# Fourteen output stores move from the sync queue to the GpSimd queue in a fused attention and maxout kernel

## The chip, the cores and the metric

The kernel runs on one core of one Trainium2 chip. The metric is the device time of one execution in microseconds; the time before is the median of three runs. The engines are named as in the profile: PE is TensorE, PEld its weight load, DVE VectorE, ACT ScalarE, POOL GpSimd, and SP the sync engine, which computes nothing and issues DMAs.

## The reference

Two layers are computed, one after the other. The first is attention for 8 batches, 8 heads, 576 tokens and a head size of 64, in which only scores near the row's maximum count:

```python
scores = scale * np.matmul(q, k.transpose(0, 1, 3, 2))
thresh = np.max(scores, axis=-1, keepdims=True) - tau      # tau = 0.02
scores = np.where(scores >= thresh, scores, -1000000000.0)
attn = np.exp(scores - np.max(scores, axis=-1, keepdims=True))
attn = attn / (np.sum(attn, axis=-1, keepdims=True) + 1e-09)
x = np.matmul(attn, v)            # then heads side by side: 4608 tokens x 512
```

The second works on the 4608 tokens with three weight matrices of 512 x 768 and one of 768 x 512:

```python
h = np.maximum(np.maximum(x @ w1, x @ w2), x @ w3)
out = h @ w_out                   # 4608 x 512, float32
```

## The kernel before

The work is cut into 16 "quads" (one batch, four heads). Each quad goes through nine chunks, and each chunk is two halves of 128 rows by 576 columns. PE makes the scores of a half in PSUM (`sc`, float32 operands `kt` and `qt` or `qs`). DVE takes a maximum or minimum of it and in the same instruction copies it into a buffer `z` in SBUF (`maximum`). ACT turns `z` into exponentials, and either ACT or DVE keeps those over the threshold and sums them (`exponents`, `numerators`). DVE inverts the two sums (`rs`). POOL multiplies each half of `z` by its `rs` into a bfloat16 tile `P` (`normalized`), which gives the `z` buffer back. When both halves of `P` are there, SP issues a DMA that transposes it into `ptq` (`turned`). When all nine chunks of a quad are turned, PE multiplies them with the values `vb` and `vrb` into `o` (`product`), and DVE or ACT copies that to `xt`.

The second layer follows one batch behind. PE makes the pieces `ph` (6 blocks of the hidden size by three matrices), ACT and DVE take their maximum (`hm`, `hT`), and PE multiplies by `w_out` into `po` (`outp`). A piece of `outp` makes two row blocks of 128 tokens; ACT copies each into one half of a tile `ob` of 128 x 2 x 512 (`done(a)`, a = 0 and 1). There are two `ob` buffers, so ACT fills one only after the store of the piece two before has landed. For whole batches one DMA then stores both halves; it writes rows of 4 KB and 512 KB in all. The function `done` does not issue it but puts it on the list `stores`. Seven of the eight batches are whole, with two pieces each, so there are 14 joined stores. The last batch is split and stores each half by itself.

Besides P, POOL casts the weights and the values (`w`, `wo`, `vb`, `vr`) and copies swapped halves of `qt` to `qs`, which PE needs for scores. SP issues nearly all DMAs: the loads of q, k and v, the weights, the 144 transposes and the stores. In the program each DMA of SP waits until the one eight before it has landed, since they share eight semaphores in turn.

The order of everything is written out by hand in the string `ORDER`, one letter per step. `S`, `T`, `O`, `F`, `N` start PE's pieces, `m`, `s`, `e`, `n`, `k`, `r` are the steps of the softmax, `p` one half of `P`, `t` its transpose, `u` the copy into `ob`, and `o` takes the next entry of the list `stores` and issues it. Each engine gets its instructions in the order of the letters (line 93 is the helper that records them, so nearly all rows of the profile have line 93) and waits only by semaphores. An instruction that waits holds up those behind it on its engine, DMA issues included. Nine buffers of `z` exist, and later two more are taken in turn from the weights' staging tiles; `P` has six.

Of the kernel before, what the change touches and what calls it, by code (L numbers as in the profile page):

```python
# [104 lines left out]
def kernel(  # L105
# [23 lines left out]
    tensor, scalar, vector, pool, sync = (  # L129
        _Ordered(tc, e) for e in (nc.tensor, nc.scalar, nc.vector, nc.gpsimd, nc.sync))  # L130
# [51 lines left out]
    def bank(name, where):  # L182
        return ps_s.tile([128, 1024], F32, name=name, tag=f"s{where}")
# [273 lines left out]
    def halves(banks):  # L457


        mine = []  # L460

        def issue(swap):
            if swap:

                gate = tensor.nop()
                tc.add_manual_dep(gate.ins, mine[0], mybir.DependencyInfo(mybir.DependencyClass.Sync, mybir.DependencyReason.DATA), reason="swap")
            for ms in zip(*banks):
                for h in (1, 0):
                    x = (1 - h) ^ swap
                    o, w, m = ms[x]  # L470
                    rows = slice(64 * h, 64 * h + 64)
                    last = tensor.matmul(o, w(rows), m(rows), start=(not swap and ms[x] is banks[x][0]),
                                         stop=(swap == 1 and ms[x] is banks[x][-1]))
            if not swap:
                mine.append(last.ins.name)

        return (lambda: issue(0)), (lambda: issue(1))

    def ffn(b, part):
# [46 lines left out]
        def outp(cs):  # L526

            my = {}
            c = cs[0]
            last = b == B - 1 and cs[-1] == 3  # L530

            def first(where):
                ps = bank("po", where)
                my["ps"] = two = [ps[:, 0:512], bank("po", (where + 2) % 4)[:, 512:1024] if last else ps[:, 512:1024]]
                if len(cs) == 1:
                    for f in range(NF):
                        tensor.matmul(ps[:, 0:512], h_of(b)[:, f, chunk_of(b, c)], wo[:, f, :],
                                      start=(f == 0), stop=(f == NF - 1))
                    return
                my["h"] = halves([[(two[a],  # L540
                                    lambda rows, a=a, f=f: h_of(b)[rows, f, chunk_of(b, c + gap * a)],
                                    lambda rows, f=f: wo[rows, f, :]) for f in range(NF)] for a in range(2)])
                my["h"][0]()

            def done(a):
                if a == 0:
                    my["ob"] = hp_.tile([128, 2, DM], F32, name="ob")
                both = my["ob"]
                ob = both[:, a]
                src = my["ps"][a]  # L550
                if last and a == 1:
                    vector.tensor_copy(out=ob, in_=src)
                    ends.append(lambda: scalar.dma_start(out=rows_out[:, (0, 2, 1, 3)[c + a]:8:4], in_=ob))
                    return
                scalar.activation(out=ob, in_=src, func=AF.Copy)
                if part is not None:
                    stores.append(lambda: sync.dma_start(out=rows_out[:, (0, 2, 1, 3)[c + a]:8:4], in_=ob))
                elif a == 1:
                    stores.append(lambda: sync.dma_start(
                        out=rows_out[:, 0:8].rearrange("p (x s a) m -> p x s (a m)", x=2, a=2)[:, :, c],  # L560
                        in_=both.rearrange("p a m -> p (a m)")))
            p = _Piece((b, "out", c), first, (lambda: my["h"][1]()) if len(cs) == 2 else None,
                       [lambda a=a: done(a) for a in range(len(cs))])
            p.kind = "uf" if last else "u"
            return p
# [76 lines left out]
    Ls, xts, stores, stores9, ends, ninths = {}, {}, [], [], [], []  # L642
# [10 lines left out]
    def h_of(b):  # L653

        return hT

    def chunk_of(b, c):
        o = S * (b % 2) + (64 if ninth_first(b) else 0) + 128 * c
        return slice(o, o + 128)
# [166 lines left out]
```

## Time and profile before

| | |
|---|---|
| time before, median of 3 runs | 447.56 us (447.33 to 448.41) |
| profiled execution, its time | 448.08 us |
| profiled execution, its span | 446.3 us |
| mean granted clock of TensorE | 0.991 |
| joined stores, issued by SP | 14, 512 KB each, 4.0 us median from issue to landing |
| transposes, issued by SP | 144, 4.2 us median to landing |
| share of DMA time on the queue of SP | 94.9% of 16 engines |

The span is the time between the first and the last instruction of the profiled execution; its time has 1.8 us more around it. Busy times are sums by engine. A row of a group gives the engine, the operation, the tile written and the tiles read, the shapes, the count, and then the busy time, the mean duration and the idle time of the engine just before. A row of the timeline gives the start, the duration, the instruction, how many of its kind follow one another, and in brackets the idle time before it with what ended it. The time in which an engine issues a DMA is not counted as busy.

### The profile page before, as it was taken

What the parts mean: (1) busy time and instruction counts of PE and PEld (TensorE: products, weight loads), DVE (VectorE), ACT (ScalarE), POOL (GpSimd) and SP (SyncE); (2) the same over time, 40 slices, a digit from 0 to 9 for tenths busy, and PEclk for the clock granted to TensorE, in tenths of its full rate; (3) what the DMA queues carried; (4) which work ended last, traced back from release to release, by engine and by line L of the source; (5) the groups of instructions that cost most, each with busy time, mean ns of one, the idle gap of its engine ahead of it and who ended that gap; (6) DMA issues with size and microseconds to landing.
All of it is one profiled execution on the core that took longest, in us unless ns stands there. A gap on an engine that the chain in (4) does not pass through costs nothing.

```text
span 446.3 us, 14304 instructions
## 1 busy us (share of the span) xinstructions
PE 421.6 (94%) x5214; PEld 319.6 (72%) x5214; DVE 393.8 (88%) x1228; ACT 403.3 (90%) x836; POOL 312.8 (70%) x420
## 2 busy tenths in 40 slices
PE   6866779999999999999999999999999999999995
PEld 5544347787788767787687777788688786787972
DVE  4788999989999999999999999998999998899541
ACT  4999999999999999999999999899999999987532
POOL 2799889979878687686785877676677676457300
PEclk9899999999999999999999999999999999999999
DMA  7999999999999999699899999989999976487723
GB/s 196 270 290 195 288 186 252 227 219 250 205 231 207 213 239 284 120 245 170 143 236 184 228 209 206 206 166 222 196 201 201 235 147 113 75 175 134 176 85 108
DMA packets 213959, 88.50 MB, mean 198 GB/s; under 512 B 189184, under 2 KB 202240, under 8 KB 213888
## 3 DMA queue, kind: packets, MB, share of 16 engines
q1 hardware_dynamic: 213360, 86.96, 94.9%
q8 instruction: 41, 0.67, 0.6%
q10 hardware_dynamic: 528, 0.62, 0.5%
q14 instruction: 30, 0.25, 0.2%
HBM read 35.65 MB, written 9.44 MB: 101 GB/s over the span
## 4 chain that ended last, share of the span: by engine, by line
PE 77%; DVE 7%; ACT 5%; DMA 4%; issue 3%; POOL 3%; SPq 0%; POOLq 0%; DVEq 0%; ACTq 0%
PE ph L93 29%; PE sc L93 26%; PE po L93 10%; PE o L93 8%; DVE z L93 5%; ACT z L93 4%; PE tp L93 3%; POOL P L93 1%; DMA vr<-in_v_dram 1%; DMA stage<-in_moe_w_dram 1%; DMA k<-in_k_dram 1%; POOL qs L93 1%; SPq L93 0%; DVE xt L93 0%; DVE hm L93 0%
## 5 line engine op out<-in xcount | busy, mean ns | idle before, releaser
L93 POOL TENSOR_SCALAR P<-z,rs 128x576 bf16<-128x576 f32 x250 | 201.0, 815 | 63.9 <-DVE rs L93 27.2
L93 DVE TENSOR_SCALAR_CACHE_REDUCE z<-sc 128x576 f32<-128x576 f32 x250 | 183.7, 750 | 14.8 <-PE sc L93 8.7
L93 PE MATMUL sc<-kt,qs 64*128 64x256 f32 (+2 forms) x640 | 180.9, 418 | 7.7 <-DVE z L93 2.4
L93 PE MATMUL sc<-kt,qt 64*128 64x320 f32 (+2 forms) x640 | 181.0, 428 | 4.8 <-ACT z L93 2.9
L93 PE MATMUL ph<-xt,w 64*128 64x288 bf16 (+2 forms) x2160 | 170.8, 283 | 0.1
L93 PEld LDWEIGHTS <-w 64*128 64x128 bf16 (+1 forms) x2160 | 129.8, 94 | 29.1 <-issue 4.7
L93 ACT ACTIVATE z<-z 128x576 f32<-128x576 f32 x174 | 117.7, 679 | 0.1
L93 PEld LDWEIGHTS sc<-kt,qs 64*128 64x128 f32 (+1 forms) x640 | 91.7, 178 | 27.2 <-DVE z L93 5.5
L93 ACT ACTIVATE z<-z,th 128x576 f32<-128x576 f32 x143 | 106.1, 768 | 5.2 <-DVE th L93 4.8
L93 PEld LDWEIGHTS sc<-kt,qt 64*128 64x128 f32 (+1 forms) x640 | 91.2, 178 | 19.2 <-ACT z L93 6.1
L93 DVE SCALAR_TENSOR_TENSOR z<-z 128x576 f32<-128x576 f32 x76 | 63.0, 840 | 0.2
L93 PE MATMUL po<-wo,hT 64*128 64x512 bf16 (+2 forms) x480 | 53.8, 355 | 0.3
L93 POOL COPY qs<-qt 64x640 f32<-64x640 f32 (+3 forms) x66 | 43.5, 660 | 10.8 <-ACT qt L93 7.2
L93 ACT ACTIVATE z<-z,nm 128x576 f32<-128x576 f32 x68 | 50.6, 767 | 0.0
L93 DVE TENSOR_TENSOR hm<-ph,hm 128x576 bf16<-128x576 f32 (+2 forms) x54 | 37.0, 686 | 9.3 <-PE ph L93 8.9
L93 ACT ACTIVATE hm<-ph 128x576 bf16<-128x576 f32 (+2 forms) x54 | 31.7, 588 | 13.5 <-PE ph L93 13.0
L93 POOL TENSOR_SCALAR P<-stage,rs 128x576 bf16<-128x576 f32 x38 | 30.3, 802 | 19.1 <-ACT z L93 5.4
L93 PEld LDWEIGHTS <-hT 64*128 64x128 bf16 (+1 forms) x480 | 29.8, 95 | 17.0 <-issue 2.5
L93 DVE TENSOR_TENSOR hT<-ph,hm 128x576 bf16<-128x576 f32 (+2 forms) x54 | 37.0, 686 | 4.0 <-PE ph L93 2.3
L93 PE MATMUL o<-ptq,vb 128*64 128x64 bf16 (+2 forms) x544 | 39.0, 281 | 0.1
L93 ACT ACTIVATION_READ_ACCUMULATOR z<-z 128x1 f32 x174 | 34.3, 197 | 0.0
L93 PEld LDWEIGHTS <-vb 128*64 128x64 bf16 x544 | 23.4, 111 | 12.9 <-issue 5.1
(45 smaller groups left out, 433.1 us busy)
## 6 DMA issues: line engine op xcount, KB each, us to landing
vm<-in_v_dram SPq DMA_DIRECT2D x32, 256.0 KB, 4.5
qm<-in_q_dram SPq DMA_DIRECT2D x15, 512.0 KB, 5.2
km<-in_k_dram SPq DMA_DIRECT2D x15, 512.0 KB, 5.2
out_dram<-ob SPq DMA_DIRECT2D x14, 512.0 KB, 4.0
stage<-in_moe_w_dram SPq DMA_DIRECT2D x9, 512.0 KB, 4.8
ptq<-P SPq DMA_TRANSPOSE x144, 4.2
vr<-in_v_dram SPq DMA_DIRECT2D x16, 128.0 KB, 3.8
stage<-in_moe_w_out_dram SPq DMA_DIRECT2D x3, 512.0 KB, 5.2
```

The source lines that it names most:

```text
L93: ins = fn(*a, **kw)
```

## The change

The joined stores are issued by POOL's queue in place of SP's. The letters of `ORDER` stay as they are, so a store now stands among POOL's instructions, where the letter `o` falls between the letters `p`, `q`, `y` and `z` of POOL, and no longer among SP's loads and transposes. The stores of the split last batch and of the ninth blocks (`ob9`) stay where they were.

```diff
                 if part is not None:
                     stores.append(lambda: sync.dma_start(out=rows_out[:, (0, 2, 1, 3)[c + a]:8:4], in_=ob))
                 elif a == 1:
-                    stores.append(lambda: sync.dma_start(
+                    stores.append(lambda: pool.dma_start(
                         out=rows_out[:, 0:8].rearrange("p (x s a) m -> p x s (a m)", x=2, a=2)[:, :, c],
                         in_=both.rearrange("p a m -> p (a m)")))
```

In the program's order POOL has 14 DMAs more and SP 14 fewer; PE, DVE and ACT keep their instructions and their order. The first store on POOL stands between the two halves of one `P`. The wait of ACT for a free `ob` buffer is now for a DMA of POOL's queue.

## The prediction

> **What bounds the kernel now.** I read the page's busy table first, then the busy time by stretch, the rows of the moved DMA, and the timelines of POOL and DVE around each place where a moved store will stand.
>
> ```profile
> PE 421.6 (94%) x5214; PEld 319.6 (72%) x5214; DVE 393.8 (88%) x1228; ACT 403.3 (90%) x836; POOL 312.8 (70%) x420
> ```
>
> ```profile
> 0.00:118.00 118.00, 99.47 (x1082) 69.16 (x1084) 102.58 (x316) 108.72 (x230) 98.22 (x132) 0.97 1.10 235
> 118.00:428.00 310.00, 308.78 (x4026) 242.45 (x4023) 284.76 (x901) 290.38 (x599) 214.56 (x289) 1.00 0.95 190
> ```
>
> The columns of the second fence are the stretch, its length, busy PE, PEld, DVE, ACT and POOL, then the PE clock, the DMA share and GB/s. All fourteen moved stores lie in the second stretch, between 120.23 and 426.64 us on SP. There PE is idle for 1.2 us of 310, so whatever delays a score or a hidden piece there pushes the end; POOL is idle for 95 us, in gaps. A store on POOL is therefore free where a gap follows it before anyone needs POOL's next output, and is paid where none does.
>
> ```profile
> L93 SPq DMA_TRANSPOSE ptq<-P x144: 1241/1426/4436, 16.8 to 419.4; - x144
> L93 SPq DMA_DIRECT2D out_dram<-ob x26: 538/602/767, 120.2 to 442.1; - x26
> L93 POOL CAST vb<-vm 128x1024 bf16<-128x1024 f32 x16 | 17.4, 1090 | 3.8 <-DMA vm<-in_v_dram 2.6 <-PE ph L93 1.1
> ```
>
> The first two rows are issues on SP's queue (min/median/max ns), the third POOL's cast of a tile of the stored tile's shape (busy us, mean ns).
>
> **What is removed.** SP loses 14 issues of 0.60 us, 8.4 us. The waits of SP's queue are 136.6 us for POOL's P (93 times), so SP mostly stands waiting for POOL, and what it gains at a store it spends at its next transpose. After 118 us PE's list of waits has none for a DMA of over 0.3 us. I cost the relief at nothing; the cover is that wait for P. What it could bring at most is POOL's waits on DMAs after 118 us, 0.6 us for `vb` and 0.6 us for a P.
>
> **What is added: one issue on POOL, 14 times.** No row of this trace shows a DMA issued by POOL. The bounds are 0.60 us (the same DMA on SP) and 1.86 us (POOL's longest P row). The nearest row of POOL's own for a full 128-partition tile is the cast, 1.03 us undisturbed (at 225.43) and 1.09 on the mean; with the 0.06 to 0.10 us that POOL leaves between two instructions of different kinds I take 1.2 us.
>
> The Trainium skill (DMA: Bandwidth & Descriptors, Specifications) gives a first byte after about 1 us on the GpSimd path and about 0.6 us on the sync and scalar path. The second figure agrees with the 0.60 us row here; the first is not shown by any run here, and taken as the issue's price it would make the sum below 0.8 us. The same page (Issuing engine by pattern) puts simple stores on Sync, which speaks against this change.
>
> **Where POOL covers it.** By the program's order I put each store behind its POOL predecessor and followed the delay to the first idle stretch of POOL, DVE or PE. Two places have little cover. Store 1 follows the P that ends at 118.65, and eight POOL instructions come with no gap but one. POOL and then DVE:
>
> ```profile
> 115.24 4.13 POOL L93 TENSOR_SCALAR P<-z,rs 128x576 bf16<-128x576 f32 x4 [0.38 <-DMA ptq<-P]
> 119.43 0.71 POOL L93 COPY qs<-qt 64x640 f32<-64x640 f32 x1
> 120.21 0.29 POOL L93 CAST vr<-vr 64x128 bf16<-64x128 f32 x1
> 120.54 0.61 POOL L93 COPY qs<-qt 64x512 f32<-64x512 f32 x1
> 121.71 0.74 POOL L93 TENSOR_SCALAR P<-z,rs 128x576 bf16<-128x576 f32 x1 [0.56 <-POOL qs L93]
> ```
>
> ```profile
> 122.49 0.75 DVE L93 TENSOR_SCALAR_CACHE_REDUCE z<-sc 128x576 f32<-128x576 f32 x1
> ...
> 124.45 0.76 DVE L93 TENSOR_SCALAR_CACHE_REDUCE z<-sc 128x576 f32<-128x576 f32 x1 [0.53 <-PE sc L93]
> ```
>
> The P of 121.71 ends at 122.45 and gives back a z buffer; the DVE row that fills it begins 0.04 us later. Of a delay, 0.4 goes into the idle 0.56 (not all of it: the `rs` that ends it also moves, since the z before it waits for POOL too), and 0.3 into DVE's idle 0.53. Cover 0.7 us.
>
> Store 4 follows the `qs` copy that ends at 192.10:
>
> ```profile
> 191.39 0.71 POOL L93 COPY qs<-qt 64x640 f32<-64x640 f32 x1
> 192.54 1.00 POOL L93 COPY qs<-qt 64x512 f32<-64x512 f32 x1 [0.45 <-ACT qt L93]
> 193.63 0.74 POOL L93 TENSOR_SCALAR P<-z,rs 128x576 bf16<-128x576 f32 x1
> ```
>
> From 192.54 to 200 POOL is nearly full. The P of 195.14 ends at 195.88, and DVE takes its z buffer at 196.08. Cover: 0.4 of the gap of 0.45 and 0.1 of the last 0.2, so 0.5 us.
>
> The others, by POOL's next idle time: store 5 has 1.01 us before 227.70 (cover 1.0); store 2 has 0.88 before 164.29 and a little on DVE (1.2); stores 9 and 10 have 0.60 and then 1.29 by 323.49, and 3.19 behind three P rows whose last frees a z that DVE takes at once at 349.08 (1.4 each). Stores 3, 6, 7, 8 and 11 stand before or close ahead of gaps of 2.43, 1.47 (and later ones), 2.00, 2.49 and 2.31 us. Stores 12 to 14 come after POOL's last P, which ends at 419.39. These eight are free up to about 2 us. New waits are short: store 1's `ob` is ready at 117.38 and store 7's at 267.22, before POOL comes; store 9's at 318.89, 0.1 us after POOL, with the P of 319.38 behind it, which waited anyway.
>
> **The sum.** At 1.2 us an issue: (1.2 − 0.7) + (1.2 − 0.5) + (1.2 − 1.0) = 0.5 + 0.7 + 0.2 = 1.4 us. At 0.60 us it is 0.1; at 1.86 us, where stores 2, 9 and 10 pay too, it is 1.16 + 1.36 + 0.86 + 0.66 + 0.46 + 0.46 = 5.0.
>
> To it comes the transfer. A store is 128 packets of 4 KB of some 160 ns, over 16 DMA engines 1.3 us of each, as before, but store 1 goes out up to 1.5 us earlier, next to transposes whose last lands 0.58 us before PE's `o` at 120.95 needs it: 0 to 0.7 us, I take 0.2. Together +1.6 us. The profiled execution took 448.08 us (span 446.3 and 1.8 around it), 0.5 above the median of 447.56; on the first this is 449.7, on the median 449.2, which I predict.
>
> **The rivals.**
> Cheap issue: POOL hands it over as fast as SP, 0.6 to 0.9 us. For it: the same 128 rows of 4 KB, the same instruction. Against: POOL's copies of 64 partitions alone take 0.60 already, and its casts 1.03. Then +0.1 to +0.7 us and the transfer's 0.2, 447.9 to 448.5, no change.
>
> Dear issue: POOL is held by DVE. The P at 168.88 takes 1.86 us instead of 0.74 while DVE runs two z<-z rows of two SBUF inputs (168.78 and 169.46). If such a DVE row holds an issue too, it takes up to 1.86 us, and the sum is 5.0 and 0 to 0.7 for the transfer: 452.6 to 453.3. Against: an issue reads no tile. The Trainium skill (SBUF — State Buffer, SBUF: two separate sides) says that DVE in a two-port mode keeps GpSimd from writing descriptors, but that DVE with two SBUF inputs is in the way only of GpSimd reads; by that, the dear case wouldn't happen here. A first issue that costs several us more, once, lands in the same place, since store 1 has only 0.7 us of cover; no other first instruction of POOL shows such a price (first P 0.74, first cast 1.04).
>
> Faster: the stores leave SP's ring, where transposes stood behind them, and SP's limit of eight DMAs in flight. If transposes then land earlier, P buffers and `vb` come sooner. For it: the store issued at 192.93 took until 199.93 to land, so the ring is crowded. Its price is POOL's 1.2 us on DMAs and PE's 1.2 idle us after 118, less the 0.1 of a cheap issue: up to 2.3 us, 445.3; say 446.0. It decides only if an issue costs under 0.7 us, and DMA waits end PE's idle time, which the list doesn't show.
>
> That the stores stay where they were is excluded by the program's order: POOL has 14 more DMAs, SP 14 fewer.
>
> **How the numbers follow.** A measurement can tell 0.3% from no change, 1.3 us. Forecast (0.95 to 1.6 us an issue, +0.9 to +3.6 with the transfer, 448.5 to 451.2): 0.52, of which 0.40 is over 1.3 us. Cheap: 0.20, no change. Dear or a costly first issue: 0.16. Faster: 0.12. So slower 0.56, same 0.32, faster 0.12. The range runs from 447.0 (the faster case lies below) to 453.2 (the dear end; a costlier first issue lies above).
>
> **What would show it.** POOL's rows should have 14 DMA issues with about 1.2 us from the end of the instruction before to the next; SP's `out_dram<-ob` 12 left. DVE's wait for POOL's P should grow by about 0.5 us near 122.5 and 0.7 near 196, with no growth at stores 3, 6 to 8 and 11. I am wrong on the price if POOL loses under 0.7 or over 1.6 us per issue, on the cover if other stores push DVE, and on the whole if PE comes out earlier at 200 us.

## The result and the profile after

The kernel with the stores on POOL takes 450.23 us (median, 449.5 to 451.75) against 447.57 us (447.33 to 448.41) for the kernel before, measured side by side: the ratio is 1.0057, with a 95% interval of 1.0033 to 1.0080. So it is slower by 0.3 to 0.8%. Its profiled execution took 449.84 us (span 448.1, mean granted clock 0.982), 1.76 us more than that of before.

The busy table, and the same second stretch as before (stretch, length, busy PE, PEld, DVE, ACT, POOL, PE clock, DMA share, GB/s):

```profile
PE 424.2 (95%) x5214; PEld 321.6 (72%) x5214; DVE 393.0 (88%) x1228; ACT 403.3 (90%) x836; POOL 320.4 (72%) x434
```

```profile
118.00:428.00 310.00, 307.37 (x4014) 241.70 (x4010) 284.64 (x900) 289.65 (x598) 222.34 (x302) 1.00 0.96 189
```

POOL has 434 rows instead of 420: the issues of this engine, unlike those of SP, are counted as busy time. PE's busy time in these 310 us is 1.4 us less (307.37 for 308.78): it stood still for that long more. The issues themselves, first the two rows that were shown of before, then POOL's new one (min/median/max ns, first and last start):

```profile
L93 SPq DMA_TRANSPOSE ptq<-P x144: 1241/1416/4269, 17.4 to 419.4; - x144
L93 SPq DMA_DIRECT2D out_dram<-ob x12: 539/588/1787, 262.4 to 443.7; - x12
L93 POOL DMA_DIRECT2D out_dram<-ob x14: 608/647/789, 118.6 to 428.6; - x14
```

A store costs POOL 0.65 us, the first one 0.79, and one directly behind another issue 0.61. Now the two places where the prediction saw the least cover. Store 1, on POOL and then on DVE:

```profile
118.56 0.79 POOL L93 DMA_DIRECT2D out_dram<-ob  x1
119.40 0.75 POOL L93 TENSOR_SCALAR P<-z,rs 128x576 bf16<-128x576 f32 x1
...
122.03 0.74 POOL L93 TENSOR_SCALAR P<-z,rs 128x576 bf16<-128x576 f32 x1
```

```profile
122.81 0.76 DVE L93 TENSOR_SCALAR_CACHE_REDUCE z<-sc 128x576 f32<-128x576 f32 x1 [0.23 <-POOL P L93]
...
124.45 0.76 DVE L93 TENSOR_SCALAR_CACHE_REDUCE z<-sc 128x576 f32<-128x576 f32 x1 [0.20 <-PE sc L93]
```

The P that stood at 121.71 is at 122.03, and the DVE row behind it at 122.81 instead of 122.49: 0.32 us late. The next such DVE row stands at 124.45 in both profiles. The delay has gone into DVE's idle time, which shrank from 0.53 to 0.20 us. Store 4, on POOL and on DVE:

```profile
192.04 0.65 POOL L93 DMA_DIRECT2D out_dram<-ob  x1
192.73 0.79 POOL L93 COPY qs<-qt 64x512 f32<-64x512 f32 x1
193.63 0.74 POOL L93 TENSOR_SCALAR P<-z,rs 128x576 bf16<-128x576 f32 x1
```

```profile
192.31 0.74 DVE L93 SCALAR_TENSOR_TENSOR z<-z 128x576 f32<-128x576 f32 x1
```

The store fits in front of a copy that begins 0.19 us later than before and takes 0.79 us instead of 1.00, so the P behind it stays at 193.63 to a hundredth. The DVE row with two inputs from SBUF runs beside the issue and does not lengthen it. Stores 6, 7 and 9 overlap such rows too, and their issues take 0.65 us as well.

To follow the whole kernel I took each PE instruction's start in this profile minus the start of the same instruction in the profile of before. This shift is 0.00 us at 121 us, -0.02 at 420 and +1.69 from 425 to the end. So eleven stores cost nothing, and everything happens at one place behind 420 us. In the stretch before it single transposes do land later than before, the one issued at 344.30 us by 3.9 us (353.19 instead of 349.28). PE reads that one only from 370 us on. PE behind 420 us, before and after:

```profile
419.75 3.88 PE L93 MATMUL ph<-xt,w 128*128 128x256 bf16 x34
423.56 0.63 PE L93 MATMUL o<-ptq,vb 128*64 128x256 bf16 x8
425.09 1.47 PE L93 MATMUL po<-wo,hT 64*128 64x512 bf16 x12
```

```profile
419.73 3.87 PE L93 MATMUL ph<-xt,w 128*128 128x256 bf16 x34
423.54 0.30 PE L93 MATMUL o<-ptq,vb 128*64 128x256 bf16 x1
425.25 0.62 PE L93 MATMUL o<-ptq,vb 128*64 128x256 bf16 x7 [1.42 <-DMA ptq<-P]
426.78 1.47 PE L93 MATMUL po<-wo,hT 64*128 64x512 bf16 x12
```

PE begins its last `o` on time, does one matmul on an older chunk, and then waits 1.42 us for the last transpose. The following `po` starts at 426.78 instead of 425.09, which is the 1.69 us. The transpose was not issued late. Here are the issues of SP's queue in the two kernels, before first, and POOL's rows after:

```profile
417.24 3.43 SPq L93 DMA_TRANSPOSE ptq<-P  x2
420.72 1.26 SPq L93 DMA_DIRECT2D out_dram<-ob  x2
```

```profile
417.21 3.53 SPq L93 DMA_TRANSPOSE ptq<-P  x2
420.83 3.30 SPq L93 DMA_DIRECT2D out_dram<-ob  x2
```

```profile
417.91 1.47 POOL L93 TENSOR_SCALAR P<-z,rs 128x576 bf16<-128x576 f32 x2 [0.72 <-POOL P L93]
419.32 1.26 POOL L93 DMA_DIRECT2D out_dram<-ob  x2
```

Before, SP issues the last transpose and only then stores 12 and 13, at 420.72 and 421.43. After, POOL has its last P behind it at 419.37 and issues the two stores at 419.32 and 419.96, while SP is still issuing the transpose (419.40 to 420.74). Both reach the DMA engines together. Landing times of the transposes issued from 417 us on, counted from the start of the issue, before and after:

```profile
DMA to landing us min/median/max: 3.2/3.2/3.2
```

```profile
DMA to landing us min/median/max: 3.2/4.5/5.8
```

The one before last takes 3.2 us in both; the last takes 5.8 instead of 3.2. From the end of its issue that is 4.47 us instead of 1.97. Of these 2.5 us the first 0.9 were to spare, because before the transpose landed at 422.64 and PE needed it at about 423.54.

The records of single DMA packets in the two traces show the same. The last transpose has 1152 packets of 256 bytes. Before, all of them start within 1.55 us (420.59 to 422.14), after, within 3.49 us (420.73 to 424.22). While the 128 packets of store 12, 4 KB each, start (420.53 to 422.00), only 97 of the transpose do; then it runs alone again, and its end meets the packets of store 13, which start from 423.28 on.

On SP the two DMAs at 420.83 are no longer stores 12 and 13 but the `ob9` stores, which SP, freed, sends early. Their first packet starts at 425.15, when all of the transpose's have started; e5 below tests them.

### The profile page after: what moved, and what is told of

It is laid out like the page before. It is cut to its first block, busy times and chain, and to the rows that moved or that the text cites. A ratio compares the mean times of both kernels' runs of the same rounds, so it can differ in the third digit from the quotient of the medians.

```text
span 448.1 us, 14305 instructions
## 1 busy us (share of the span) xinstructions
PE 424.2 (95%) x5214; PEld 321.6 (72%) x5214; DVE 393.0 (88%) x1228; ACT 403.3 (90%) x836; POOL 320.4 (72%) x434
## 4 chain that ended last, share of the span: by engine, by line
PE 84%; DVE 5%; ACT 3%; issue 3%; DMA 3%; SPq 1%; POOL 0%; DVEq 0%; ACTq 0%
PE sc L93 32%; PE ph L93 30%; PE po L93 10%; PE o L93 9%; DVE z L93 4%; PE tp L93 3%; ACT z L93 3%; DMA ptq<-P 1%; DMA qm<-in_q_dram 1%; SPq L93 1%; POOL P L93 0%; DVE xt L93 0%; DVE hm L93 0%; ACT qt L93 0%; DVE stage L93 0%
## 5 line engine op out<-in xcount | busy, mean ns | idle before, releaser
L93 PE MATMUL sc<-kt,qs 64*128 64x256 f32 (+2 forms) x640 | 183.0, 423 | 5.5 <-DVE z L93 2.2
L93 PE MATMUL sc<-kt,qt 64*128 64x320 f32 (+2 forms) x640 | 183.4, 434 | 4.5 <-ACT z L93 2.3
L93 PEld LDWEIGHTS sc<-kt,qt 64*128 64x128 f32 (+1 forms) x640 | 92.2, 180 | 18.9 <-ACT z L93 5.0
```

Source lines behind the costliest of these rows:

```text
L93: ins = fn(*a, **kw)
```

## The experiments

Theory A is the reading above: the loss is the last transpose, slowed by the two stores issued beside it, and nothing else. Theory B keeps the forecast's cause, the issues on POOL or their transfers, but spreads it: the loss comes from many places of the full stretch, in sizes too small to see singly. The kernels of the first four experiments ran together, beside 35 runs of the kernel before (median 448.24 us), the other three beside 26 (448.55 us). The shift of PE in the first 100 us differs from one profile to the next by up to 2.7 us, where no edit lies, so I compare the steps that the shift makes behind 118 us.

| kernel | stores on POOL | median us | ratio (95%) | step of PE's shift, 420 to 425 us | last transpose, issue's end to landing, us |
|---|---|---|---|---|---|
| before | none | 447.57 | | | 1.97 |
| after | 14 | 450.23 | 1.0057 (1.0033 to 1.0080) | 1.7 | 4.47 |
| e1_first11 | 1 to 11 | 448.64 | 1.0004 (0.9980 to 1.0029) | 0.0 | 1.94 |
| e2_last3 | 12 to 14 | 450.67 | 1.0062 (1.0037 to 1.0086) | 2.05 | 4.88 |
| e3_split | 1 to 11, two issues each | 449.80 | 1.0032 (1.0009 to 1.0055) | 0.0 | 1.91 |
| e4_sync_before_t | none | 449.95 | 1.0038 (1.0011 to 1.0066) | 1.2 | 2.50 |
| e5_earlier | 14, 12 and 13 earlier | 448.05 | 0.9998 (0.9982 to 1.0013) | 0.0 | 1.94 |
| e6_one | 12 only | 448.41 | 1.0003 (0.9988 to 1.0019) | 0.84 | 3.67 |
| e8_after_again | 14 | 449.95 | 1.0044 (1.0026 to 1.0061) | 2.19 | 4.95 |

**e1_first11: only the first eleven stores on POOL.**

```diff
-                    stores.append(lambda: sync.dma_start(
+                    e = pool if 2 * b + c < 11 else sync
+                    stores.append(lambda: e.dma_start(
```

> Stores 1 to 11 on POOL, 12 to 14 on SP as before. Theory A (the last transpose shares the DMA engines with stores 12 and 13, and nothing else is lost): as before, 447.6 us (447.0 to 448.3); the last transpose lands about 2.0 us after its issue. Theory B (the issues on POOL, or their transfers on a queue of their own, cost a little in many places): about the changed kernel's 450, at least 449. By the forecast's cover table with the issue measured at 0.65 us: +0.15 us, the same as A.

It is as fast as before, within 0.3%. The issue is the same as in the full change, eleven times:

```profile
L93 POOL DMA_DIRECT2D out_dram<-ob x11: 647/650/792, 120.4 to 395.1; - x11
```

PE's shift against before is +1.86 us at 121, at 420 and at the end: no step at any store. The +1.86 come from the first 100 us. This fits theory A and not B.

**e2_last3: only the last three on POOL.**

```diff
-                    stores.append(lambda: sync.dma_start(
+                    e = sync if 2 * b + c < 11 else pool
+                    stores.append(lambda: e.dma_start(
```

> Stores 12 to 14 on POOL, 1 to 11 on SP. Theory A: the changed kernel's loss comes back whole, 449.3 to 451.0; PE waits 1.4 to 2 us for the last transpose at 423.5. Theory B: 447.6 to 448.3.

These three alone give the whole loss, 1.0062. PE's row in the list of waits (sum, times, longest):

```profile
PE o L93 <- DMA ptq<-P: 1.8, 1, 1.8
```

There is one such wait, as in the full change (1.4). Together e1 and e2 settle where the time goes.

**e3_split: a dearer issue in the full stretch.** Each of stores 1 to 11 goes out as two DMAs of 64 partitions, so that POOL pays about the 1.2 us of the forecast. Stores 12 to 14 stay on SP.

```diff
-                    stores.append(lambda: sync.dma_start(
-                        out=rows_out[:, 0:8].rearrange("p (x s a) m -> p x s (a m)", x=2, a=2)[:, :, c],
-                        in_=both.rearrange("p a m -> p (a m)")))
+                    out_of = rows_out[:, 0:8].rearrange("p (x s a) m -> p x s (a m)", x=2, a=2)[:, :, c]
+                    in_of = both.rearrange("p a m -> p (a m)")
+
+                    def twice():
+                        if 2 * b + c >= 11:
+                            sync.dma_start(out=out_of, in_=in_of)
+                            return
+                        for h in range(2):
+                            pool.dma_start(out=out_of[32 * h:32 * h + 32], in_=in_of[64 * h:64 * h + 64])
+                    stores.append(twice)
```

> As the first kernel of this call, but each of the stores 1 to 11 is cut into two DMAs of 64 partitions on POOL, so that POOL has two issues in each place. If a half costs the 0.65 us of a whole, the cover table of the forecast gives at 1.3 us an issue (1.3-0.7)+(1.3-0.5)+(1.3-1.0)+(1.3-1.2) = 1.8 us: 449.4. If a half costs 0.35, nothing: 447.6. If the table is too strict: no loss though POOL's rows show 1.3 us in each place.

A half takes 0.55 to 0.60 us, so a place costs from 1.14 (store 5, 226.76 to the next row at 227.91) to 1.33 us (store 1, whose first half took 0.74). The kernel is slower by 0.3%, and PE's shift now has steps in the stretch: +0.38 at store 1, +0.07 at store 2, +0.24 at store 4, +0.11 between 265 and 283 us, +0.47 at store 9 and +0.13 at store 10, together 1.4 us. With these prices the forecast's table gives about 1.5 us: 0.6 at store 1, 0.7 at store 4, 0.15 at store 5 and nothing elsewhere. So its total was nearly right, but not its places: stores 1 and 4 cost less, store 5 nothing, and store 9 the most. What happened at store 9, POOL and then DVE of this kernel, then DVE of the kernel before:

```profile
319.64 1.15 POOL L93 DMA_DIRECT2D out_dram<-ob  x2 [0.40 <-ACT ob L93]
...
322.59 0.74 POOL L93 TENSOR_SCALAR P<-z,rs 128x576 bf16<-128x576 f32 x1
```

```profile
322.70 1.23 DVE L93 SCALAR_TENSOR_TENSOR z<-z 128x576 f32<-128x576 f32 x1
```

```profile
322.25 0.75 DVE L93 SCALAR_TENSOR_TENSOR z<-z 128x576 f32<-128x576 f32 x1
```

Delayed by the issue, POOL's P now runs at the same time as DVE's row with two inputs from SBUF, and that row takes 1.23 us instead of 0.75. The delay moved a collision, which a table of idle gaps doesn't hold. So POOL's issues do cost PE time at a price of 1.14 to 1.33 us a place; at the real 0.65 us they cost nothing.

**e4_sync_before_t: the same order of arrival, on SP.** In the kernel before, the letters of stores 12 and 13 move ahead of the last `t`.

```diff
- 2tvF3vF1hF2voF3vF1ohF2vF3vF1hF2vO3...
+ 2ootvF3vF1hF2vF3vF1hF2vF3vF1hF2vO3...
```

> All stores on SP as before, but the letters of stores 12 and 13 stand ahead of the last transpose in the written order. If it is the place ahead of the last transpose that costs, whatever the queue: two issues of 0.62 us and the two stores' packets come first, the last transpose lands 1.25 us later by the issues and 1.3 to 2.6 later by the data; with 0.9 us to spare before PE needs it, +1.6 to +3.0 us, 449.2 to 450.6. If only the second queue beside SP's costs: the issues alone, +0.3 us, 447.9.

SP's issues:

```profile
419.45 1.28 SPq L93 DMA_TRANSPOSE ptq<-P  x1
420.78 1.25 SPq L93 DMA_DIRECT2D out_dram<-ob  x2
422.12 2.31 SPq L93 DMA_TRANSPOSE ptq<-P  x1
```

PE waits 0.92 us for the last transpose, and the step is 1.2 us; the kernel is 0.4% slower. The step is less than the 1.6 us expected at least. The delay comes by another way than in the full change: the transpose is issued 0.5 us later than before (422.12, less the shift of 2.2 us that stands there, against 419.42), its issue takes 2.31 us instead of 1.28, and from the issue's end it lands in 2.50 us, 0.5 us more than before. Its packets start at 424.86, when those of the two stores have started. So it is the lost place of the transpose ahead of the stores that costs, on either queue; how the loss divides between issue and transfer depends on the queue.

This profile also has a step of 0.77 us near 290 us, where nothing was changed and which no other profile shows. POOL's cast of `vb` there starts at 291.17, 0.01 us ahead of a DVE row with two SBUF inputs, and that row takes 1.63 us instead of 0.75. In the kernel before the cast starts 0.14 us behind the same row and takes 1.51 us itself. The ratio may hold some of this step, which has nothing to do with the stores' place.

**e5_earlier: all fourteen on POOL, stores 12 and 13 out of the transpose's way.** Store 12 follows directly behind store 11, store 13 goes into POOL's gap ahead of the P of 415.7.

```diff
-1sevyS2terBmpeF3svS1iyepBmoS0yhm...
+1sevyS2terBmpeF3svS1iyepBmooS0yhm...
-...kpemBkperumO2uptO3xpN1wtenk...
+...kpemBkperumO2uptO3xpoN1wtenk...
- 2tvF3vF1hF2voF3vF1ohF2vF3vF1hF2vO3...
+ 2tvF3vF1hF2vF3vF1hF2vF3vF1hF2vO3...
```

> All 14 stores on POOL, with the letters of two of them earlier: store 12 right behind store 11 (near 394 us, its ob is ready at 372.8), store 13 in POOL's idle time before 415.7, ahead of it three P. Theory A (the packets of stores 12 and 13 share the DMA engines with the last transpose): both have landed before the last transpose is issued, which lands about 2.0 us after its issue again; as before, ratio 0.998 to 1.002. Rival: SP, freed of the three stores, sends the two ob9 stores right behind the last transpose (420.8 instead of 427.2), and these or the queue of POOL as such delay it: then PE still waits 1.4 us or more at 423.5, ratio 1.004 to 1.006.

The loss is gone, with all fourteen issues on POOL: 0.9998. Store 13's issue, and the last transpose's landing from the start of its issue:

```profile
413.46 0.65 POOL L93 DMA_DIRECT2D out_dram<-ob  x1
```

```profile
DMA to landing us min/median/max: 3.2/3.2/3.2
```

SP sends the two `ob9` stores directly behind the last transpose here too, and it still lands in 3.2 us:

```profile
419.96 1.18 SPq L93 DMA_DIRECT2D out_dram<-ob  x2
```

That clears them, and it clears POOL's queue as such. What remains is that stores 12 and 13 are in flight at that moment. Store 13 slows a transpose here too, the one issued at 413.54, which lands after 5.3 us (418.83); but PE begins its `o` only at 422.71, so this costs nothing.

**e6_one: one store beside the transpose.** Of all fourteen, only store 12 goes to POOL.

```diff
-                    stores.append(lambda: sync.dma_start(
+                    e = pool if 2 * b + c == 11 else sync
+                    stores.append(lambda: e.dma_start(
```

> Only store 12 on POOL, all others on SP as before. Theory A, by size: one store is 128 packets of 0.16 us on 16 engines, 1.3 us of each; the last transpose lands 1.3 us later (3.3 us after its issue) and PE has 0.9 us to spare: +0.4 us, ratio 1.000 to 1.002. If it is not the bytes but that any POOL store is open beside a transpose: the transpose lands as late as with two stores (4.5 to 4.9 us) and the ratio is 1.004.

```profile
DMA to landing us min/median/max: 4.9/4.9/4.9
```

```profile
PE o L93 <- DMA ptq<-P: 0.5, 1, 0.5
```

From its issue's end the transpose lands in 3.67 us, between the 1.97 us without a store beside it and the 4.5 to 4.95 with two, and the step in PE's shift is 0.84 us, two fifths to a half of the full one. Both are more than was expected (3.3 us and 0.4 us). The time itself (1.0003, up to 1.0019) cannot tell 0.84 us from nothing, so the dose rests on the profile alone.

**e8_after_again: the full change once more.**

> The changed kernel again, beside the two above on the same chip: ratio 1.004 to 1.008; the shift of PE against the kernel before stays level from 118 to 420 us and steps up by 1.6 to 2.1 us at 423.5.

Slower again, by 0.3 to 0.6%. PE waits 1.9 us for the last transpose, and the shift is -0.50 at 121 and at 420 us and +1.69 at the end: no step up to 420 us, then 2.19. The first profile was no accident, and steps of 1.7 to 2.2 us are 0.4 to 0.5% of the time, within the interval of both ratios. No version beat the kernel before by more than the noise.

## Why the prediction was right, and for the wrong reason

The forecast was 449.2 us and slower; it is 450.23 and slower. The number came out near by another way than the one it was built on, and that is luck: 1.4 us were forecast for POOL's issues, which cost nothing, and nothing for the last transpose, which cost 1.7 to 2.2 us.

**The relief of SP, at nothing: right.** e1 and e5 take 11 and 14 issues from SP and gain nothing that can be measured. Some transposes do land earlier, the last one for the `o` at 120.95 at 117.79 instead of 120.37, but PE was not waiting for them.

**1.2 us an issue: wrong, too high by 0.55.** The price is 0.65 us, near the low bound (0.60, the same DMA on SP). I chose the cast as nearest because it is POOL's own and has the tile's shape; the row with the same operation on another engine was the nearer one. Nor did the 0.06 to 0.10 us for a change of kind come on top: the issue's row begins 0.05 us before the one ahead ends. The times to a first byte were the wrong thing to set beside a price: store 12's first packet starts 1.21 us after its issue began, and POOL was free after 0.65. The rival "cheap issue" had this price right.

**The cover: right at the real price, roughly right at the assumed one.** By the prediction's own table 0.65 us leaves 0.15 us at store 4, and the first issue's 0.79 leaves 0.1 at store 1; PE's shift at 420 us is -0.02. DVE's waits for POOL's P did not grow:

```profile
DVE z L93 <- POOL P L93: 2.0, 6, 0.8
```

Before they were longer:

```profile
DVE z L93 <- POOL P L93: 4.2, 8, 0.8
```

Near 122.5, where the wait was to grow by 0.5 us, DVE was 0.32 us late, and the 0.7 near 196 did not come. e3, at about the assumed price, lost 1.4 us in the stretch, as in the sum. That the totals agree is partly luck, since 0.47 us of it came at store 9 by a collision that the table could not hold.

**"Stores 12 to 14 come after POOL's last P ... free": the step that failed.** It is right for POOL, which nobody waits for there, and wrong for the kernel. I asked who waits for POOL behind a moved store, but, except at store 1, not when the store would now start and what would be in flight then. On SP these stores stood behind the last transpose and could not start before it; POOL, with nothing left to do, reaches them 1.4 us earlier. All of the 1.7 to 2.2 us lies here (e2 has it, e1 and e5 don't).

**The transfer term: right in size, at the wrong place.** A store was put at 1.3 us of each DMA engine, from its packets. Two are 2.6 us, less 0.9 to spare 1.7, which is the step of the first profile; the landing grew by 2.5 to 3.0 us. With one store it grew by 1.7, so the packet estimate is a little low for the first. I applied the term to store 1 alone, at 0 to 0.7 us, where no step was seen: the last transpose before that `o` had landed at 117.79, ahead of the store's issue at 118.56.

The Trainium skill (DMA: Bandwidth & Descriptors, Queues, rings and completion order) says that a DMA engine takes turns between the queues it has work for, packet by packet. The trace agrees: beside store 12 packets of the two start by turns in the sum over the engines (97 of 256 bytes for 128 of 4 KB), and the transpose is late by about the stores' whole time. The same page (Issuing engines are not separate DMA queues) holds that issuing from several engines only saves the issuer's time; here even that saving gained nothing, and the transpose lost its start ahead of the stores.

**The rivals.** Dear issue: refuted by stores 4, 6, 7 and 9, whose issues took 0.65 us beside DVE's two-input rows, and by the first issue's 0.79 us. The rule of the Trainium skill weighed there (SBUF — State Buffer, SBUF: two separate sides), that two SBUF inputs hold up only GpSimd's reads, held at these four. Cheap issue: right on the price, and its "no change" is what e1 and e5 gave. It did not give this kernel's loss, since it too had the transfer at store 1 only. Faster: not seen; PE's waits had no DMA to gain from.

## What to carry to other kernels

Moving a DMA to another queue moves it in time as well, and out of the order that the first queue gave. Beside the issuing engine's gaps, list for each moved DMA when the new issuer reaches it, and what with a reader close behind is then in flight; a small-packet transpose with 0.9 us to spare is lost to two 512 KB stores. Where stores must go to another queue, place them where no such transfer is near its reader: e5 did that with two letters and was as fast as before.

## What the runs showed of the hardware

POOL issues a DMA of 128 rows of 4 KB in 0.65 us, one of 64 rows in 0.55 to 0.60, and the first of a program in 0.79 (0.74 for a half). A DVE row with two SBUF inputs beside it did not lengthen it (four cases). POOL's instructions that read SBUF do collide with such a row, and in the three cases named here the one that started first kept its time: the row took 1.23 us behind a P (e3) and 1.63 behind a cast (e4) instead of 0.75, and in the kernel before, the cast, starting second, took 1.51 instead of 1.04. From issue to landing the stores took 5.5 us (median) on POOL's queue against 4.0 on SP's, in the same kernel otherwise:

```profile
out_dram<-ob POOLq DMA_DIRECT2D x14, 512.0 KB, 5.5
```

On POOL's queue a store's first packet starts 1.2 to 5.4 us after the start of its issue. Whether that is the queue or the company they keep there was not tried. In e5 it is 5.5 too, and that kernel is no slower; its list of waits has none for these stores' landing. While the packets of store 12 started, the transpose of the other queue got 97 packets of 256 bytes in for the store's 128 of 4 KB. Last, a transpose issued behind two stores on the same queue took 2.31 us to issue instead of 1.28 and landed 0.5 us later after that (e4).
